# One more pair of token tiles by seven products in a linear-attention and SwiGLU kernel, with the small work around it moved between engines

## The chip, the core and the metric

The kernel runs on one core of a Trainium2 chip. The core has a matrix engine (TensorE, PE in the profile; its weight loads are shown apart as PEld), three engines for element-wise work (VectorE = DVE, ScalarE = ACT, GpSimd = POOL), and SyncE (SP), which only issues transfers here. Each engine works through its own list of instructions in order; semaphores make one engine wait for another. Matrix products land in PSUM, all other tiles lie in SBUF, and inputs, outputs and spill buffers in HBM.

The metric is the device time of one execution in microseconds (us): 748.28 for the kernel before, the median of three runs (747.86 to 748.52).

## The reference

`x` is 2048 tokens by 1024. It is normalised, and two blocks use the result: a linear attention with 32 heads of 32 columns, and a feed-forward block with a hidden width of 3584.

```python
xn = layernorm(x)                                    # over the 1024 columns, no weights
q, k, v = split(xn @ wqkv)                           # 32 heads of 32 columns each
phi = lambda t: where(t > 0, t + 1, exp(t)) + 1e-6
kv, z = sum_s phi(k)[s] (x) v[s],  sum_s phi(k)[s]   # per head: 32x32 and 32
num, den = phi(q) @ kv,  phi(q) . z + 1e-6
s = (num / den) @ wo
g = silu((silu(xn @ w_gate) * (xn @ w_up)) @ w_down)
out = x + s * g
```

The `1e-6` that is added to `den` is one of the operations that the change touches; `@ wo` is the output projection that it touches most.

## The kernel before

Tokens are handled in 16 tiles of 128, four tiles to a block of 512 (`TB`). The stages follow each other on TensorE:

1. Normalisation, keys and values (to about 155 us). Products of 128x128 weights with 512 columns; `kvz_ps` gathers `kv` and `z` of all heads.
2. Queries of the second half of the tokens (class `QGroup`, groups `qa`, `qb`, `qc`), woven into the start of stage 3. Each query group needs its results passed through `exp` and `relu` on ScalarE (`emit_exp_relu`, L186 and L187, four instructions per half group) and through a minimum and an addition on VectorE (`emit_phi`, L190 and L191, called by `part_d`, a "row").
3. num/den and output projection (about 156 to 232 us). For each of the 16 token tiles `nd_tile()` calls `emit_ND` (L779), and for each of 32 half rows `s_unit()` calls `emit_S` (L821).
4. The feed-forward block (from 232 us): groups of gate and up products (class `Group`), then the down projection.

Most large products are done in blocks of two by two with seven products in place of eight (the names `M1` to `M5`, `N6`, `N7`), which needs sums of the operands' blocks ahead (on VectorE) and three combining additions behind. A group has three parts: `part_a` computes `M3` into `X` and `M4` into `Y`, copies `X` to SBUF on ScalarE and adds `Y` on VectorE; `part_b` computes `M1` into `Z`, which is added to that sum, then accumulates `M5` onto `X` and `M2` onto `Y`; `part_c` accumulates `N7` and `N6` and subtracts. So `M5` may start only when the copy of `X` is done, and `M2` only when the addition has read `Y`.

What `emit_ND` issues for one tile: 8 products of 132 columns into three PSUM tiles `nd_ps` (three, three and two head groups), of which the pool `psA` has three buffers in all, so that the next call writes the same three; per PSUM tile an addition of 1e-6 to the denominators into `rden` (L794, VectorE); one reciprocal of `rden` (L797, VectorE); and per PSUM tile a multiplication into `o_sb` (L800, VectorE). `emit_OT` then stores `o_sb` to `o_dram` from ScalarE's queue (L815) and issues a transposing load into `oT` from SyncE's queue (L816); behind the last tile it also issues the first six weight loads of the feed-forward block (`load_w`, L177 and L179).

`emit_S` multiplies one transposed tile with half of `wo` (8 products of 512 columns), copies the result on ScalarE (L833) and, for the second half, stores the row to `s_dram` from ScalarE's queue (L836).

The last four token tiles are projected by seven products: class `SGroup` takes two tiles, its `sums()` makes four sums of their transposes on VectorE, and five sums of blocks of `wo` (`wo_sums`, 128x2048 each) are made once, on GpSimd (L959). The places for these sums are reused ones: halves of `oT` blocks whose tiles have been projected, and the upper half of `ws_all`.

The order around the change is written out by hand. The block at L921 runs under `manual_schedule` for TensorE, VectorE, ScalarE, GpSimd and SyncE, so each engine's list is the order in which the Python code emits. Before the loop come three `nd_tile()` calls between the parts of `qa` and `qb`, each followed by an `emit_OT()`. The loop over `u` counts the output-projection units; at each `u` it looks up whether a query part (`q_at`), a num/den tile (`nd_at`), a row (`row_at`), a sum of `wo` (`wo_at`) or the sums of the first group (`sum_at`) goes with it, then calls `s_unit()` and `emit_OT()`. In the feed-forward block only TensorE and GpSimd keep the written order; VectorE and ScalarE are ordered by the planner, and `gate(...)` ties an instruction behind another in that planning, without a semaphore unless `sync=True`. `sum_w(m, gu)` makes the four sums of a feed-forward weight block on VectorE (L152 to L155); `sum_w(0, 0)` and `sum_w(0, 1)` stand at the end of the block at L921.

Of the kernel before, what the change touches and what calls it, by code (L numbers as in the profile page):

```python
# [9 lines left out]
ACT = mybir.ActivationFunctionType  # L10
ALU = mybir.AluOpType
# [10 lines left out]
def kernel(  # L22
# [143 lines left out]
    def sum_w(m, gu):  # L166
        wsum[(m, gu)] = ws_all[:, m % 2, gu]
        for op in wsum_ops(wraw[(m, gu)], wsum[(m, gu)]):
            op()

# [18 lines left out]
    def emit_phi(dst, e):  # L189
        nc.vector.tensor_scalar(out=e, in0=e, scalar1=1.0, scalar2=EPS, op0=ALU.min, op1=ALU.add)  # L190
        marks["phi"] = nc.vector.tensor_tensor(out=dst, in0=e, in1=dst, op=ALU.add)  # L191

# [563 lines left out]
    with ExitStack() as p2:  # L756
        wop = p2.enter_context(tc.tile_pool(name="wop", bufs=1, reuse_waits="tile"))
        otp = p2.enter_context(tc.tile_pool(name="p2oT", bufs=1))
        work = p2.enter_context(tc.tile_pool(name="p2work", bufs=2))
        small = p2.enter_context(tc.tile_pool(name="p2small", bufs=2))  # L760
        oT_ab = otp.tile([P, 2, G, TB], BF16, name="oT")
        oT_cd = wq_sb[:].rearrange("p c n -> p (c n)").rearrange("p (b g t) -> p b g t", b=2, t=TB)
# [3 lines left out]
        def oT_of(b):  # L766
            return (oT_ab[:] if b < 2 else oT_cd)[:, b % 2]
# [11 lines left out]
        def emit_ND(b, t):  # L779
# [4 lines left out]
            for j in range(NJ):  # L784
                g0 = j * GPT
                ng = min(GPT, G - g0)
                nd_ps = psA.tile([P, GPT, NDW], FP32, name="nd_ps", tag="A")
                for gi in range(ng):
                    g = g0 + gi
                    mm = nc.tensor.matmul(nd_ps[:, gi, :], lhsT=pqT_tiles[(p, g // 2)][:, g % 2, t0:t0 + P],  # L790
                                          rhs=KVZ[:, g, :], start=True, stop=True)
                    if j == 0 and gi == 0 and t == 0:
                        marks[("ND", b)] = mm
                nc.vector.tensor_scalar(out=rden[:, g0:g0 + ng, :], in0=nd_ps[:, 0:ng, P:P + HPG],  # L794
                                        scalar1=EPS, scalar2=None, op0=ALU.add)
                nds.append((g0, ng, nd_ps))
# [13 lines left out]

        def emit_OT():
            while o_ready:
                b, t, o_sb = o_ready.popleft()
# [7 lines left out]
        def emit_S(b, t, cc):  # L821
# [12 lines left out]
            if cc == NCC - 1:  # L834
# [9 lines left out]
        wos += [oT_ab[:, 1, 0:HD]]  # L844
        wo_sums = deque((out, u, v, op) for out, (u, v, op) in zip(wos, (
            (w12, w22, ALU.subtract), (w21, w11, ALU.subtract), (w11, w22, ALU.add), (w21, w22, ALU.add),
# [4 lines left out]
                  oT_cd[:, 0, 0:1].rearrange("p a (k c) -> p (a k) c", k=HD)]  # L851
        o_sums = [oT_ab[:, 1, HD:DC], oT_cd[:, 0, HD:DC]]

        class SGroup:


            def __init__(self, t):
                self.t = t
                o = oT_of(NB - 1)[:, :, t * P:(t + 2) * P]
                a, b = o[:, :, 0:P], o[:, :, P:2 * P]  # L860
                self.o, self.s1, self.sum = o, o_sum1[t // 2], o_sums[t // 2]
                s1, sm = self.s1, self.sum
# [19 lines left out]
            def store(self, i):  # L882
                r0 = ((NB - 1) * TPB + self.t + i) * P
                nc.scalar.dma_start(out=s_dram[r0:r0 + P, :], in_=self.s[i][:])
# [32 lines left out]
        def nd_tile():  # L917
            if nds:
                emit_ND(*nds.popleft())

        with tc.manual_schedule(engines=FRONT_ORDER | {ET.SP}):  # L921
# [18 lines left out]
            rows = deque((grp, i) for grp in (qa, qb, qc) for i in range(2))  # L940
            nd_at = {1, 2, 4, 6, 8, 10, 11, 13, 15, 16, 17, 19, 20}
            row_at = {0, 1, 3, 5, 7, 9}
            wo_at = {10, 11, 12, 14, 18}
            sum_at = {23: lambda: groups[0].sums()}
            q_at = {0: qc.part_a, 2: qc.part_b, 3: qc.part_c}
            assert len(nd_at) == len(nds) and len(row_at) == len(rows)
            n7 = TPB * NCC
            groups = [SGroup(t) for t in range(0, TPB, 2)]
            for u in range(len(units) - n7):
                if u in q_at:  # L950
                    q_at[u]()
                if u in nd_at:
                    nd_tile()
                if u in row_at:
                    grp, i = rows.popleft()
                    grp.part_d(i)
                if u in wo_at:
                    out, a, b, op = wo_sums.popleft()
                    gate([nc.gpsimd.tensor_tensor(out=out, in0=a, in1=b, op=op)], marks["phi"], sync=True)  # L959
                if u in sum_at:  # L960
                    sum_at[u]()
                s_unit()
                emit_OT()
            sg, sh = groups
            sg.part_a()
            sh.sums()
            sg.part_b()
# [4 lines left out]
            sh.part_c()  # L972
            sum_w(0, 1)
    p12.close()
# [209 lines left out]
    with tc.manual_schedule(engines=PE_ORDER):  # L1184
        prev = None
        for m, p in order:
# [15 lines left out]
            for gu in range(2):  # L1202
# [14 lines left out]
                grp.part_b()  # L1217
                prev = grp
                if p == 0 and m + 1 < NM:
                    sum_w(m + 1, gu)  # L1220
                if gu == 0 and (m, p) in wd_at:
# [126 lines left out]
```

## Time and profile before

| | before |
|---|---|
| median of 3 runs | 748.28 us (747.86 to 748.52) |
| profiled execution | 747.96 us |
| its span, first to last instruction | 746.2 us |
| granted TensorE clock | 0.999 |

The work of the engines by stretch of the span, in us of busy time (the profile's table by stretches):

| stretch, us | PE | DVE | ACT | POOL | DMA share |
|---|---|---|---|---|---|
| 0 to 70, normalisation, keys and values | 68.08 | 57.15 | 32.41 | 14.04 | 0.78 |
| 70 to 143, the same with query groups | 72.69 | 58.60 | 43.82 | 0 | 0.01 |
| 143 to 161 | 17.95 | 14.40 | 10.01 | 0 | 0.38 |
| 161 to 212, num/den and projection | 50.68 | 39.67 | 22.10 | 20.13 | 0.65 |
| 212 to 232, last projection groups | 19.89 | 12.64 | 6.43 | 0 | 0.97 |
| 232 to 400, feed-forward | 167.17 | 125.45 | 65.13 | 0 | 0.53 |
| 400 to 568 | 168.00 | 119.38 | 65.02 | 0 | 0.57 |
| 568 to 746.2, down projection and end | 172.45 | 90.14 | 27.37 | 35.74 | 0.45 |

A line of the timeline has the start in us, the duration, engine, source line, operation, the tiles written and read, their sizes and the number of instructions that the line merges; in brackets stands how long the engine was idle before it and what ended that. Matmuls overlap: four of 512 columns that follow each other start 0.216 us apart, though each is listed with 0.38 us. A few matmul records are missing, so that a merged line can count 7 where 8 ran. "ACTq" and "SPq" are the queues' issue of transfers.

### The profile page before, as it was taken

The numbers are of one execution on the slowest core, as the hardware profiler recorded it, in microseconds if no ns is written. First come the engines' busy times: TensorE is split into PE (matmuls) and PEld (weight loads), VectorE is DVE, ScalarE is ACT, GpSimd is POOL, SyncE is SP. The second block draws the span as 40 slices with busy tenths as digits, with TensorE's granted clock in tenths as the row PEclk, the third lists the DMA queues.
The fourth block names the chain that finished last, engine by engine and source line by source line (L and its number), as shares of the span: only waits on it lengthen the run. The fifth ranks groups of instructions, "written<-read, shape, count | busy, mean of one in ns | idle before, by whom it ended". The sixth has DMA issues, their size and how long they took to land.

```text
span 746.2 us, 9886 instructions
## 1 busy us (share of the span) xinstructions
PE 736.9 (99%) x3661; PEld 347.0 (47%) x3700; DVE 517.4 (69%) x955; ACT 272.3 (36%) x476; POOL 69.9 (9%) x106
## 2 busy tenths in 40 slices
PE   9999999999999999999999999999999999999997
PEld 4544444455544444444444444444444444444454
DVE  6889896688768767787678867776655754445554
ACT  4444574755223343434343333434342111111111
POOL 3210000000730000000000000000000221121220
PEclk9999999999999999999999999999999999999999
DMA  9756000316689553655337643455779745554200
GB/s 313 260 161 170 1 0 1 113 44 156 198 230 278 149 149 101 188 174 158 109 97 204 184 127 105 150 161 156 265 255 344 284 171 183 184 184 170 98 29 29
DMA packets 132464, 118.09 MB, mean 158 GB/s; under 512 B 33728, under 2 KB 112704, under 8 KB 131136
## 3 DMA queue, kind: packets, MB, share of 16 engines
q1 hardware_dynamic: 127520, 108.68, 47.1%
q10 hardware_dynamic: 4896, 8.78, 3.5%
q8 instruction: 29, 0.48, 0.3%
q14 instruction: 19, 0.16, 0.1%
HBM read 70.52 MB, written 39.58 MB: 148 GB/s over the span
## 4 chain that ended last, share of the span: by engine, by line
PE 96%; DMA 2%; DVE 1%; issue 0%; ACT 0%; DVEq 0%; ACTq 0%
PE X L131 29%; PE Y L131 29%; PE Z L131 10%; PE kv_ps L455 9%; PE s_ps L829 5%; PE qX L131 3%; PE qY L131 3%; PE kY L131 2%; PE kX L131 2%; DMA wg_sb<-in_B_w_gate_dram 1%; PE nd_ps L790 1%; PE kvz L484 1%; PE qZ L131 1%; PE kZ L131 1%; DMA xp<-in_A_x_dram 0%
## 5 line engine op out<-in xcount | busy, mean ns | idle before, releaser
L131 PEld LDWEIGHTS <-ws_all 128*128 128x128 bf16 x1424 | 138.1, 98 | 164.0 <-issue 1.9
L1011 DVE TENSOR_TENSOR q<-n,Y 128x512 f32<-128x512 f32 x63 | 43.3, 688 | 104.4 <-PE Y L131 103.2
L131 PEld LDWEIGHTS <-xs 128*128 128x128 bf16 (+1 forms) x736 | 69.6, 98 | 76.5
L1281 POOL TENSOR_TENSOR o_out<-y,xres 128x512 bf16<-128x512 f32 x29 | 35.1, 1210 | 495.1 <-DVE y L1280 495.1
L131 PE MATMUL Y<-xs,ws_all 128*128 128x512 f16 (+3 forms) x308 | 70.3, 360 | 0.0
L131 PE MATMUL X<-xnT,ws_all 128*128 128x512 f16 (+1 forms) x278 | 70.1, 379 | 0.2
L131 PE MATMUL Y<-xnT,ws_all 128*128 128x512 f16 x224 | 57.5, 379 | 0.8 <-DVE q L1011 0.8
L131 PE MATMUL X<-xs,ws_all 128*128 128x512 f16 x224 | 57.5, 379 | 0.0
L131 PE MATMUL Z<-xs,ws_all 128*128 128x512 f16 x224 | 57.5, 379 | 0.0
L1135 ACT ACTIVATE g<-cg 128x512 bf16<-128x512 f32 x56 | 35.3, 630 | 54.4 <-DVE cg L1026 54.4
L1017 DVE TENSOR_TENSOR u<-Z,q 128x512 f32<-128x512 f32 x63 | 43.2, 686 | 15.9 <-PE Z L131 15.9
L1135 ACT ACTIVATE g<-X 128x512 bf16<-128x512 f32 x28 | 16.7, 597 | 99.0 <-PE X L131 99.0
L1007 ACT COPY n<-X 128x512 f32<-128x512 f32 x63 | 36.9, 585 | 30.8 <-PE X L131 27.6
L455 PEld LDWEIGHTS <-xnT 128*128 128x128 f16 x320 | 30.7, 98 | 36.0 <-DVE xnT L427 0.5
L1160 DVE TENSOR_TENSOR ho<-g,up 128x1024 bf16<-128x1024 bf16 x56 | 38.2, 685 | 0.5
L455 PE MATMUL kv_ps<-wk_sb,xnT 128*128 128x512 bf16 x156 | 36.9, 379 | 0.6 <-DVE xnT L427 0.3
L1280 DVE TENSOR_TENSOR y<-y,s_in 128x512 f32<-128x512 f32 x31 | 22.2, 717 | 21.4 <-ACT y L1274 15.8
L455 PE MATMUL kv_ps<-wv_sb,xnT 128*128 128x512 bf16 x155 | 35.9, 379 | 0.2
L131 PEld LDWEIGHTS <-wu_sb 128*128 128x128 bf16 x224 | 21.9, 98 | 26.4
L131 PEld LDWEIGHTS <-wg_sb 128*128 128x128 bf16 x224 | 21.9, 98 | 26.4
L1274 ACT ACTIVATE y<-X 128x512 f32<-128x512 f32 x8 | 4.8, 597 | 69.7 <-PE X L131 61.2
L829 PE MATMUL s_ps<-wo_sb,oT 128*128 128x512 bf16 x123 | 29.0, 379 | 0.2
(208 smaller groups left out, 1146.8 us busy)
## 6 DMA issues: line engine op xcount, KB each, us to landing
h_dram<-ho SPq DMA_DIRECT2D x56, 256.0 KB, 2.5
wg_sb<-in_B_w_gate_dram SPq DMA_DIRECT2D x14, 512.0 KB, 4.0
wu_sb<-in_B_w_up_dram SPq DMA_DIRECT2D x14, 512.0 KB, 4.4
wdr<-in_B_w_down_dram SPq DMA_DIRECT2D x14, 512.0 KB, 4.2
ws_all<-h_dram SPq DMA_DIRECT2D x4, 1792.0 KB, 8.7
wds_dram<-wdsA SPq DMA_DIRECT2D x14, 384.0 KB, 2.7
hp_a<-h_dram SPq DMA_DIRECT2D x3, 1792.0 KB, 9.6
o_dram<-o_sb ACTq DMA_DIRECT2D x16, 256.0 KB, 3.1
```

Source lines behind the costliest of these rows:

```text
L131: marks["mm"] = nc.tensor.matmul(acc[:, 0:c1 - c0], lhsT=lhs(k), rhs=rhs(k)[:, c0:c1], start=(first and k == 0), stop=(k == n - 1), skip_g ...
L455: mm = nc.tensor.matmul(kv_ps[:], lhsT=xn_tok_ap(i)[:, dc, :], rhs=wkv_ap(c)[:, dc, :], start=(dc == 0), stop=(dc == DC - 1))
L484: nc.tensor.matmul(kvz_ps[j][:, gi, 0:P + 1], lhsT=pk_sb[:, g * P:(g + 1) * P], rhs=v_sb[:, g, 0:P + 1], start=(i == 0 and gi == 0), stop= ...
L790: mm = nc.tensor.matmul(nd_ps[:, gi, :], lhsT=pqT_tiles[(p, g // 2)][:, g % 2, t0:t0 + P], rhs=KVZ[:, g, :], start=True, stop=True)
L829: mm = nc.tensor.matmul(s_ps[:], lhsT=oT[:, c, ttok], rhs=wo_sb[:, c, cc * CW:(cc + 1) * CW], start=(c == 0), stop=(c == G - 1))
L1007: nc.scalar.copy(out=n[:], in_=self.X[:])
L1011: nc.vector.tensor_tensor(out=self.q[:], in0=n[:], in1=self.Y[:], op=ALU.add)
L1017: nc.vector.tensor_tensor(out=self.u[:], in0=Z[:], in1=self.q[:], op=ALU.add)
L1135: nc.scalar.activation(out=self.g[:, i, j * TB:(j + 1) * TB], in_=src, func=ACT.Silu)
L1160: nc.vector.tensor_tensor(out=self.ho[:, i], in0=self.g[:, i], in1=self.up[:, i], op=ALU.mult)
L1280: nc.vector.tensor_tensor(out=t[:], in0=t[:], in1=self.s_in[:, i, cs], op=ALU.mult)
L1281: (nc.vector if last and (i, j) != (0, 0) else nc.gpsimd).tensor_tensor(out=self.o_out[:, i, cs], in0=t[:], in1=self.xres[:, i, cs], op=AL ...
```

## The change

Five things are changed together.

- The projection of the third last pair of token tiles (tiles 10 and 11) is done by `SGroup` as well: `S7 = 3` groups in place of two, so 20 units remain in the loop in place of 24. The three groups are called `sf`, `sg`, `sh`. The places for their sums alternate between two.
- The 1e-6 is added to the denominators on ScalarE: an `activation` with function `Identity` and a bias tile `eps_nd`, which GpSimd fills once.
- The five sums of `wo` are made on VectorE, at other units (`wo_at`), and without the `gate` to the last row.
- The num/den tiles and the rows come at other units (`nd_at`, `row_at`), the last tile at `u` = 18 of 20 in place of 20 of 24; `emit_OT` moves from behind `s_unit()` to behind `nd_tile()`, and there handles only the tiles that were ready before that `nd_tile()`.
- `sum_w(0, 1)` moves out of the block into the feed-forward loop, behind `part_b` of the first group, and it and both `sum_w(1, gu)` are gated behind the last matmul issued there.

```diff
     def sum_w(m, gu):
         wsum[(m, gu)] = ws_all[:, m % 2, gu]
-        for op in wsum_ops(wraw[(m, gu)], wsum[(m, gu)]):
-            op()
+        return [op() for op in wsum_ops(wraw[(m, gu)], wsum[(m, gu)])]
...
+        eps_nd = small.tile([P, 1], FP32, name="eps_nd", tag="eps_nd", bufs=1)
+        nc.gpsimd.memset(eps_nd[:], EPS)
...
-                nc.vector.tensor_scalar(out=rden[:, g0:g0 + ng, :], in0=nd_ps[:, 0:ng, P:P + HPG],
-                                        scalar1=EPS, scalar2=None, op0=ALU.add)
+                nc.scalar.activation(out=rden[:, g0:g0 + ng, :], in_=nd_ps[:, 0:ng, P:P + HPG], func=ACT.Identity,
+                                     bias=eps_nd[:])
...
-        def emit_OT():
-            while o_ready:
+        def emit_OT(n=None):
+            for _ in range(len(o_ready) if n is None else n):
...
+        S7 = 3
...
-            def __init__(self, t):
-                self.t = t
-                o = oT_of(NB - 1)[:, :, t * P:(t + 2) * P]
+            def __init__(self, n):
+                self.t = NT - 2 * (S7 - n)
+                t = self.t % TPB
+                o = oT_of(self.t // TPB)[:, :, t * P:(t + 2) * P]
                 a, b = o[:, :, 0:P], o[:, :, P:2 * P]
-                self.o, self.s1, self.sum = o, o_sum1[t // 2], o_sums[t // 2]
+                self.o, self.s1, self.sum = o, o_sum1[n % 2], o_sums[n % 2]
...
-            nd_at = {1, 2, 4, 6, 8, 10, 11, 13, 15, 16, 17, 19, 20}
-            row_at = {0, 1, 3, 5, 7, 9}
-            wo_at = {10, 11, 12, 14, 18}
-            sum_at = {23: lambda: groups[0].sums()}
+            nd_at = {1, 2, 4, 5, 7, 9, 10, 11, 13, 14, 15, 17, 18}
+            row_at = {0, 1, 3, 5, 6, 8}
             q_at = {0: qc.part_a, 2: qc.part_b, 3: qc.part_c}
+            wo_at = {6: (2,), 8: (3,), 12: (0,), 16: (1, 4)}
...
+                done = len(o_ready)
                 if u in nd_at:
                     nd_tile()
+                emit_OT(done)
                 if u in row_at:
                     grp, i = rows.popleft()
                     grp.part_d(i)
-                if u in wo_at:
-                    out, a, b, op = wo_sums.popleft()
-                    gate([nc.gpsimd.tensor_tensor(out=out, in0=a, in1=b, op=op)], marks["phi"], sync=True)
-                if u in sum_at:
-                    sum_at[u]()
+                for k in wo_at.get(u, ()):
+                    out, a, b, op = wo_sums[k]
+                    nc.vector.tensor_tensor(out=out, in0=a, in1=b, op=op)
+                if u == len(s_order) - 1:
+                    groups[0].sums()
                 s_unit()
-                emit_OT()
-            sg, sh = groups
+            sf, sg, sh = groups
+            sf.part_a()
+            sg.sums()
+            sf.part_b()
             sg.part_a()
+            sf.part_c()
             sh.sums()
             sg.part_b()
             sh.part_a()
             sg.part_c()
             sum_w(0, 0)
             sh.part_b()
             sh.part_c()
-            sum_w(0, 1)
...
                 grp.part_b()
                 prev = grp
+                if (m, p, gu) == (0, 0, 0):
+                    gate(sum_w(0, 1), marks["mm"])
                 if p == 0 and m + 1 < NM:
-                    sum_w(m + 1, gu)
+                    sums = sum_w(m + 1, gu)
+                    if m == 0:
+                        gate(sums, marks["mm"])
```

## The prediction

> **What bounds the kernel now.** I read the page's busy times and its chain first, then TensorE's waits, then the timeline of 156 to 238 us, where the change lies.
>
> ```profile
> PE 736.9 (99%) x3661; PEld 347.0 (47%) x3700; DVE 517.4 (69%) x955; ACT 272.3 (36%) x476; POOL 69.9 (9%) x106
> PE 96%; DMA 2%; DVE 1%; issue 0%; ACT 0%; DVEq 0%; ACTq 0%
> ```
>
> TensorE bounds every stage. So a product that goes is worth its own spacing, and work on another engine costs nothing until TensorE waits for it: the question is which wait is new. TensorE waits for little today; the largest wait is at the start of the feed-forward block:
>
> ```profile
> 232.93 1.03 PE L131 MATMUL Y<-xs,wg_sb 128*128 128x512 f16 x4
> 233.91 1.02 PE L131 MATMUL Z<-xs,ws_all 128*128 128x512 f16 x4
> 234.30 0.58 ACT L1007 COPY n<-X 128x512 f32<-128x512 f32 x1 [3.25 <-PE Y L131]
> 234.94 1.02 PE L131 MATMUL X<-xnT,ws_all 128*128 128x512 f16 x4
> 236.05 0.68 DVE L1011 TENSOR_TENSOR q<-n,Y 128x512 f32<-128x512 f32 x1
> 236.79 1.02 PE L131 MATMUL Y<-xnT,ws_all 128*128 128x512 f16 x4 [0.83 <-DVE q L1011]
> ```
>
> Four matmuls follow each other in 4 x 0.216 = 0.86 us; here the three products come 0.12, 0.17 and 0.99 us late, 1.27 in all. VectorE reaches `q` late because sums of feed-forward weights (L152 to L155) stand ahead of it.
>
> The num/den tiles are tight too. TensorE's next tile writes the `nd_ps` buffers that VectorE's multiplications of this one read:
>
> ```profile
> 160.43 0.63 PE L790 MATMUL nd_ps<-KVZ,pqT 128*128 128x132 bf16 x8
> 160.49 0.63 ACT L186 ACTIVATE e_t<-pqT 128x512 bf16<-128x512 bf16 x1 [1.86 <-DVE pqT L251]
> 161.24 0.31 DVE L794 TENSOR_SCALAR rden<-nd_ps 128x12 f32<-128x12 f32 x3
> 161.97 1.35 DVE L800 TENSOR_TENSOR o_sb<-nd_ps,rden 128x384 bf16<-128x384 f32 x3
> 162.33 0.63 ACT L187 ACTIVATE pqT<-pqT 128x512 bf16<-128x512 bf16 x1
> 163.49 0.63 PE L790 MATMUL nd_ps<-KVZ,pqT 128*128 128x132 bf16 x8
> ```
>
> Tile 1's multiplications end at 163.32, 0.17 us ahead of tile 2's products. And ScalarE, which is to add the 1e-6, is busy with the query group's four exp/relu until 162.96. Where two tiles stand one unit apart, TensorE waits already (0.77 in place of 0.63 us), and ScalarE copies and stores the previous unit in between:
>
> ```profile
> 203.83 0.77 PE L790 MATMUL nd_ps<-KVZ,pqT 128*128 128x132 bf16 x8
> 204.03 0.58 ACT L833 CAST s_sb<-s_ps 128x512 bf16<-128x512 f32 x1 [1.61 <-PE s_ps L829]
> 204.20 0.59 DVE L794 TENSOR_SCALAR rden<-nd_ps 128x12 f32<-128x12 f32 x3
> 204.64 0.33 ACTq L836 DMA_DIRECT2D s_dram<-s_sb  x1
> 205.22 1.35 DVE L800 TENSOR_TENSOR o_sb<-nd_ps,rden 128x384 bf16<-128x384 f32 x3
> 206.15 0.76 PE L790 MATMUL nd_ps<-KVZ,pqT 128*128 128x132 bf16 x8
> ```
>
> **The change part by part.** Order on each engine is the code's own.
>
> *Third pair by seven products.* 32 matmuls become 28: -4 x 0.216 = -0.86 us. Its sums and combining steps (four sums, 1.7 us; three additions and two subtractions in place of copies) run on VectorE beside 6 us of products each. `sg.sums` overwrites places that `sf.part_a` reads, and is needed 6 us later; `sh` writes the `s_sb` buffers that `sf` stores from, whose stores go out 8 us before; stores at 227.78 us landed after 5.8. So 0 here; if the store is late ScalarE's copy waits, and behind it the next product (a rival below).
>
> *Weight sums later.* `q` and `u` come ahead of the eight sums (3.3 us), which are needed about 4 us after `u` at the earliest: the 1.27 us go, -1.27. Weight loads are issued behind the last transposing load; from tile 15's num/den to the feed-forward block TensorE now has 19.7 us (212.40 to 232.07), then about 21.6, so SyncE's queue is earlier and hides them.
>
> *1e-6 on ScalarE.* 48 instructions leave VectorE (0.46 us a tile) and 48 come to ScalarE. No row shows this operation there. The nearest is the square root of 128x1 from SBUF with a bias tile, 0.296 us; exp of 128x512 takes 0.63 from SBUF and 0.597 from PSUM, so I take 0.26 for PSUM, and 0.16 from start to start, since exps from PSUM follow each other at 0.495, 0.10 under their length. Ends: VectorE's 0.17 and 0.12 for the same operation; 0.296 without overlap. GpSimd's memset waits for buffers of the stage before; ScalarE's first use is at 157.8, 2 us after anything it can wait for.
>
> By the Trainium skill, "ScalarE: Activation LUTs", section "What ACT_TABLE_LOAD costs", an activation with a bias pointer takes about 280 ns + 0.833 ns a column and overlaps the next by 93 ns: 0.29 and 0.197 us as an estimate; by it the whole sum would be +5.9 in place of +5.1 us. The 0.296 row agrees with it; the two exp rows, 33 ns apart, do not let me use it unchanged for PSUM.
>
> More than its length it is the place that costs. Replaying the rows' durations in the new order:
>
> Tile 2. Tile 0's additions now follow ScalarE's relu that starts at 157.29: 157.8 to 158.4, reciprocal at 158.4, not 157.38. VectorE is 1.0 late, so the query group's subtractions and ScalarE's four exp/relu are too: they start at 161.5 and pass at 163.9. Only then come tile 1's additions: reciprocal 164.5 (was 161.59), multiplications ending 165.45, 165.9 and 166.25. Tile 2's products, due at 163.49, run at 165.5 to 166.4 in place of ending at 163.99: +2.45 us.
>
> Tile 6, now one unit behind tile 5 (2.2 us, was 3.9). In ScalarE's list tile 5's additions stand behind `qc`'s four exp/relu, the copy of unit 3 and its store: with the rows at 178 to 181.4 that is 2.2 us behind tile 5's first product. Additions 0.58, reciprocal 0.35, multiplications 0.56, 0.47, 0.42 more; tile 6's third buffer is free at +4.5, due at +2.55: +1.99 us.
>
> Tile 8 needs the last query row. Row and tile 8 keep their distances of one unit to tile 7 and to each other, which left 0.18 us (191.28 to 191.46). Tile 7's additions follow a copy and the sum of `wo` at unit 6 (1.22 us): +0.69 on the last products.
>
> Tiles 9, 10, 12, 13 and 15 stand one unit behind another. For 12: ScalarE's copy ends 0.78 behind tile 11's first product, additions 0.78 to 1.36, reciprocal to 1.75, multiplications to 2.35, 2.8 and 3.15; the buffers are due at 2.2, 2.37 and 2.55: +0.65. In the same way 9, 10, 13 and 15 come to 0.59, 0.48, 0.41 and 0.65; together +2.78.
>
> Today's waits in this stretch go, since the sums above count from the undelayed spacing: four of 0.126 at num/den tiles, and 0.19 at `qb`'s `N7` and `N6`: -0.69.
>
> *Sums of wo on VectorE.* 5 x 1.22 us (the 128x2048 rows at L510) in place of 5 x 4.07 on GpSimd, off TensorE's path but for the part in tile 8 above; the two at unit 16 end ahead of tile 14's reciprocal.
>
> *Order of stores.* `o_sb` stores now stand behind the next tile's additions, about 0.7 us later on ScalarE's queue; transposing loads on SyncE's follow them. Tiles 10 and 11 are read 14 us or more after their products; tile 13 was read from SBUF after 11 today. 0; without that cover a late transposition would stop TensorE one for one.
>
> Sum: -0.86 - 1.27 - 0.69 + 2.45 + 1.99 + 0.69 + 2.78 = +5.09. The profiled execution took 747.96 us (span 746.2 and 1.76 around it): 753.05, and the median of the runs stands 0.32 above it: 753.4. With the low price of an addition the same replay gives +3.8, with the high one +7.3: 752.1 to 755.6.
>
> **Rivals.** *Faster:* the additions on ScalarE end no later than VectorE's did, 0.87 us after a tile's first product. Then the 0.46 us that VectorE saves cover the rest and only the savings stay: -2.82, 745.5. It decides if ScalarE's backlog ahead of tiles 1 and 5 is gone when their products end; the rows at 160.49 to 162.96 speak against it.
>
> *Half:* an addition costs 0.1 us and 0.05 from start to start: +2.3, 750.6. Every row on ScalarE speaks against it.
>
> *No change:* the pile-ups behind exp/relu (tiles 2 and 6) hide, the pairs cost what I say: 5.09 - 4.44 = +0.65, 748.9.
>
> *More:* TensorE's gaps of 2 us bring its clock down. At the start of the span matmuls follow each other 0.427 us apart for 3.2 us; eight such more per gap, 0.211 each, at two gaps: +3.4, 756.8. Against it: the 0.99 us wait at 236.79 is followed by 0.216 spacing. By the Trainium skill, "TensorE: Matmul & The Clock Gate", Part 1, the clock halves after an idle window of about 3.4 us, and no gap here is so long. A late `sf` store, 1 us, would end in the same region.
>
> **How the numbers follow.** Mine 0.75; faster 0.07; half 0.06; no change 0.05; more 0.07. Changes within 0.2% (1.5 us) count as none, which is about what a measurement can tell here. Faster 0.07, same 0.05, slower 0.88. The range 750.5 to 756.0 takes in the ends of the addition's price and the half case, and leaves out the rest, under 0.2.
>
> **What would show it.** Right: in the changed profile TensorE waits for `o_sb` at L790's line, over 1.5 us at tiles 2 and 6; `rden` on ScalarE starts behind L187; no wait for `q` at the first feed-forward group; the stretch from 156 us to the first `M3` of the feed-forward block longer by 6.4 us. Wrong: `rden` well under 0.2 us, or ScalarE free when the products of tiles 1 and 5 end.

## The result and the profile after

The changed kernel took 755.88 us in the median of six executions (753.57 to 760.25) against 748.37 us for the kernel before beside it. The ratio is 1.0111, with an interval of 1.0092 to 1.013: slower by 1.1%, which on the 748.28 us of the table is 756.6 us. The forecast was 753.4 us with a range up to 756.0. The direction was right; the size was not, by 3 us.

The recorded profile is that of the fastest of the six: 753.57 us, span 751.8 us, 5.61 us more than the profiled execution before. The forecast for a profiled execution was 753.05. So the profile shows an execution in which the forecast sum came out nearly as worked, and the typical execution has some 2 us more that this profile does not show. Both halves need an explanation.

The page of the changed kernel, busy times and chain:

```profile
PE 738.2 (98%) x3658; PEld 346.0 (46%) x3696; DVE 520.3 (69%) x920; ACT 280.6 (37%) x523; POOL 50.0 (7%) x102
PE 94%; DVE 3%; ACT 2%; issue 1%; ACTq 0%; DVEq 0%
```

TensorE still bounds the span, but VectorE and ScalarE now hold 5% of the chain (1% before), and 1% is issue. The waits of TensorE in the same profile (columns: what waited, for whom, us in total, times, longest):

```profile
PE nd_ps L791 <- DVE o_sb L801: 3.9, 2, 2.0
PE nd_ps L791 <- DVE pqT L190: 0.4, 1, 0.4
```

The two long waits are those of tiles 2 and 6. The timeline at tile 1 and tile 2 (start, duration, engine, line, operation, tiles):

```profile
160.21 0.63 PE L791 MATMUL nd_ps<-KVZ,pqT 128*128 128x132 bf16 x8
...
163.07 0.63 ACT L186 ACTIVATE pqT<-pqT 128x512 bf16<-128x512 bf16 x1
163.61 0.57 ACT L795 ACTIVATE rden<-nd_ps,eps_nd 128x12 f32<-128x12 f32 x3
...
164.21 0.35 DVE L798 RECIPROCAL rden<-rden 128x32 f32<-128x32 f32 x1 [2.42 <-ACT rden L795]
...
164.67 1.35 DVE L801 TENSOR_TENSOR o_sb<-nd_ps,rden 128x384 bf16<-128x384 f32 x3
...
165.28 1.08 PE L791 MATMUL nd_ps<-KVZ,pqT 128*128 128x132 bf16 x8 [1.85 <-DVE o_sb L801]
```

Tile 1's products start at 160.21, but its additions follow the query group's last relu and start 3.4 us later; before, VectorE had added 0.81 us behind the products (160.43 to 161.24). VectorE sits idle 2.42 us for `rden`, and tile 2's products come 2.44 us late (2.016 us ahead of the first, 0.278 and 0.150 between the groups). The pair that was shown before, tiles 11 and 12, in the timeline after:

```profile
206.90 1.09 PE L791 MATMUL nd_ps<-KVZ,pqT 128*128 128x132 bf16 x8
206.92 0.58 ACT L834 CAST s_sb<-s_ps 128x512 bf16<-128x512 f32 x1 [1.12 <-PE s_ps L830]
207.54 0.33 ACTq L837 DMA_DIRECT2D s_dram<-s_sb  x1
207.92 0.27 ACT L795 ACTIVATE rden<-nd_ps,eps_nd 128x12 f32<-128x12 f32 x1 [0.41 <-PE nd_ps L791]
...
208.99 1.35 DVE L801 TENSOR_TENSOR o_sb<-nd_ps,rden 128x384 bf16<-128x384 f32 x3
209.60 1.09 PE L791 MATMUL nd_ps<-KVZ,pqT 128*128 128x132 bf16 x8
```

Eight matmuls that took 0.77 us now take 1.09, and the next tile comes 2.70 us after this one where it came after 2.32 us. The start of the feed-forward block:

```profile
240.19 0.58 ACT L1015 COPY n<-X 128x512 f32<-128x512 f32 x1 [2.27 <-PE X L131]
240.66 1.03 PE L131 MATMUL Z<-xs,ws_all 128*128 128x512 f16 x4
240.93 0.69 DVE L1019 TENSOR_TENSOR q<-n,Y 128x512 f32<-128x512 f32 x1 [1.19 <-PE Y L131]
241.52 1.03 PE L131 MATMUL X<-xnT,ws_all 128*128 128x512 f16 x4
242.38 1.03 PE L131 MATMUL Y<-xnT,ws_all 128*128 128x512 f16 x4
```

`q` ends at 241.62, 0.76 us ahead of the product that writes `Y` again; before, that product started 0.06 us behind `q`, after a wait of 0.83. Now the products follow each other at 0.86 us.

By stretch, from TensorE's starts in the two profiles: up to the first num/den products nothing moved (149.29 and 149.27 us from the first key/value products); from there to the feed-forward block's first product 75.56 became 82.56, +7.00; from there to the last matmul 509.27 became 508.09, -1.18.

### The profile page after: what moved, and what is told of

Same layout as the page of the kernel before. It is cut to its first block, busy times and chain, and to the rows that moved or that the text cites. A ratio compares the mean times of both kernels' runs of the same rounds, so it can differ in the third digit from the quotient of the medians.

```text
span 751.8 us, 9888 instructions
## 1 busy us (share of the span) xinstructions
PE 738.2 (98%) x3658; PEld 346.0 (46%) x3696; DVE 520.3 (69%) x920; ACT 280.6 (37%) x523; POOL 50.0 (7%) x102
## 4 chain that ended last, share of the span: by engine, by line
PE 94%; DVE 3%; ACT 2%; issue 1%; ACTq 0%; DVEq 0%
PE X L131 29%; PE Y L131 29%; PE Z L131 10%; PE kv_ps L454 9%; PE s_ps L830 3%; PE qY L131 2%; PE qX L131 2%; PE kY L131 2%; PE kX L131 2%; DVE o_sb L801 1%; PE sX L131 1%; PE sY L131 1%; PE kvz L483 1%; PE qZ L131 1%; PE w_ps L492 1%; PE nd_ps L791 1%
```

## The experiments

The forecast's theory is that the additions on ScalarE are the whole loss, by what stands ahead of them in ScalarE's order. What it left open after the result is the part beyond the profile. The theory for that is the rival "More": long gaps halve TensorE's clock for a while, in some executions and not in others. Its own rival was a late store. In all runs below the kernel before ran beside them: 747.84 us in the median for the first four (23 executions), 747.96 for the next four (17, from the one longer gap to the version with the stores later), 747.86 for the last three (21).

### The changed kernel again

No edit.

> The changed kernel unchanged, for more executions with their granted clocks. The recorded profile was the fastest of six executions (753.57 us, clock 1.000); the other five took 754.47 to 760.25 at 0.999 to 0.995. Theory A (the two gaps of about 2.5 us at num/den tiles 2 and 6 bring TensorE's clock down in some executions): the fastest executions stand at 753 to 754 with clock 1.000, the others above by (1 - clock) x 752 us, and a profile with a lower clock shows it low right behind 165 or 186 us. Theory B (late transposing loads or weight loads make the spread): the times spread at a clock of 1.000, and the profile shows waits for DMA on TensorE.

755.58 us (754.45 to 759.5); ratio 1.0109, interval 1.0091 to 1.0128. This time the profile is of a 756.40 us execution, and it has what the first had not. The table by stretches (us; busy time and instructions of each engine; granted clock; DMA), four neighbouring stretches around tile 2's products:

```profile
core 0: us, PE busy (x) PEld busy (x) DVE busy (x) ACT busy (x) POOL busy (x), PEclk, DMA share, GB/s
160.60:164.00 3.40, 3.40 (x23) 1.77 (x22) 2.17 (x5) 1.77 (x3) 0.00 (x0) 1.00 0.24 81
164.00:167.40 3.40, 1.43 (x12) 0.58 (x11) 2.11 (x5) 3.06 (x9) 0.00 (x0) 1.00 0.18 42
167.40:170.80 3.40, 3.40 (x10) 1.20 (x9) 2.69 (x7) 0.91 (x4) 0.00 (x0) 0.50 0.70 118
170.80:174.20 3.40, 3.40 (x19) 1.63 (x18) 1.23 (x3) 2.56 (x5) 0.00 (x0) 1.00 0.58 154
```

Behind the stretch in which TensorE stood for tile 2, the granted clock is 0.50 for 3.413 us, and then 1.00 again. Matmuls of 512 columns follow each other 0.427 us apart there in place of 0.216; eight fit, so one such stretch costs 8 x 0.211 = 1.7 us. The profile of the first run had the same gap and no such stretch. Against that first profile the way from tile 0 to the feed-forward block is 1.87 us longer: 1.7 for the clock, 0.77 for a wait at 239.97 us (below), less 0.64 that tile 6's wait is shorter, since TensorE reaches it later. The start of the program took 1.1 us more as well, ahead of everything that the change touches: the granted clock first rises at 6.98 us here and at 4.73 in the first profile. So the clock is the largest part of the 2.8 us between the two executions, and not all of it.

### 1e-6 back on VectorE

```diff
-        eps_nd = small.tile([P, 1], FP32, name="eps_nd", tag="eps_nd", bufs=1)
-        nc.gpsimd.memset(eps_nd[:], EPS)
...
-                nc.scalar.activation(out=rden[:, g0:g0 + ng, :], in_=nd_ps[:, 0:ng, P:P + HPG], func=ACT.Identity,
-                                     bias=eps_nd[:])
+                nc.vector.tensor_scalar(out=rden[:, g0:g0 + ng, :], in0=nd_ps[:, 0:ng, P:P + HPG],
+                                        scalar1=EPS, scalar2=None, op0=ALU.add)
```

> The changed kernel with one part undone: the 1e-6 is added on VectorE again. No backlog of exp/relu lies ahead of the additions. Theory A: the gaps at tiles 2 and 6 go; what is left are about 1.0 at tile 8, 1.0 at tile 9 and 0.65 at tile 15 from the sums of wo on VectorE, +0.6 against the kernel before (748.9 us), with a clock of 0.999 to 1.000 in every execution. Theory B: the spread of several us stays, since loads and stores are as they were.

748.51 us (748.08 to 753.29); ratio 1.0016, interval 1.0005 to 1.0027. One part of the change makes 7.1 of the 7.7 us. Tile 2 has no wait left, and tile 6 one of 0.12 us, as four tiles of the kernel before have. What is left besides is 0.46 us at tile 15, and 0.78 at tile 8 and 0.98 at tile 9, where VectorE now does two sums of `wo`, 1.22 us each, right at the last query row.

The profile fell on the slowest of the twelve executions, 753.29 us, and shows a wait that the prediction had priced at nothing. The timeline at the third group of the projection, with the same columns:

```profile
228.83 2.11 SPq L178 DMA_DIRECT2D wu_sb<-in_B_w_up_dram  x1
...
231.28 3.17 ACTq L885 DMA_DIRECT2D s_dram<-s_sb  x2
...
234.54 0.58 ACT L902 CAST s_sb<-sX 128x512 bf16<-128x512 f32 x1 [6.43 <-DMA wu_sb<-in_B_w_up_dram]
...
235.18 1.47 PE L131 MATMUL sX<-ws_all,oT 128*128 128x512 bf16 x4 [2.51 <-ACT s_sb L902]
```

`sg`'s two stores stand on ScalarE's queue ahead of `sh`'s copies. The second is not issued until 234.12, just behind the landing of a load of feed-forward weights at 234.02: in the program's list of waits the store and the load share a semaphore, since transfers take these in turn. `sh`'s copy stands behind the store and `sh`'s `N7` behind the copy, 2.67 us late. And that gap halves the clock (table by stretches, columns as above):

```profile
232.20:235.60 3.40, 0.89 (x5) 0.29 (x3) 0.81 (x2) 1.06 (x2) 0.00 (x0) 1.00 1.20 300
235.60:239.00 3.40, 3.40 (x10) 1.19 (x8) 1.30 (x2) 0.02 (x1) 0.00 (x0) 0.50 1.12 341
```

In the profile of the changed kernel run again the same wait is the 0.77 us at 239.97; in its first profile it is absent. It depends on when a load lands, so it differs by execution.

### The additions on ScalarE for the early or for the late tiles only

```diff
+                if b * TPB + t >= 7:
                     nc.scalar.activation(...)
+                else:
+                    nc.vector.tensor_scalar(...)
```

> The changed kernel with the 1e-6 on VectorE for tiles 0 to 6 and on ScalarE from tile 7 on: no query group's exp/relu stand ahead of any ScalarE addition. Theory A: the two long gaps go, the short ones (0.4 to 0.65 us at tiles 8, 9, 10, 12, 13, 15, 3.2 in all) stay; +0.9 against the kernel before, 749.2 us, and the clock holds at 0.999 to 1.000. If many short gaps bring the clock down rather than two long ones, this spreads as the changed kernel does. Theory B: spreads.

> The complement: the 1e-6 on ScalarE for tiles 0 to 5, on VectorE from tile 6 on. Theory A: the two long gaps stay (about 2.45 and 2.2 us at tiles 2 and 6); fastest executions at +4.7, 753.0 us, the others higher by up to 6 us at clocks of 0.995 to 0.999, as with the changed kernel. If short gaps do it: the clock holds and all executions stand within 1 us of 753.0.

Here the late tiles are 7 to 15, the early ones 0 to 5 (with `< 6`). Late tiles only: 749.29 us (748.99 to 750.29), ratio 1.0023, interval 1.0015 to 1.0032; no single gap of over 0.51 us behind the first num/den product, and no half clock before the last matmul. Early tiles only: 754.5 us (753.25 to 754.78), ratio 1.0086, interval 1.0073 to 1.0099; 2.45 us at tile 2, 1.96 at tile 6, and in the profiled execution (754.66 us) a stretch of 3.413 us at half clock behind tile 2. Against the additions wholly on VectorE the late tiles add 0.8 us and the early ones 6.0. The early ones' two waits are worth 4.4; the stretch at half clock, 1.7, makes 6.1. The four executions do not all fit this: one took 754.34 us at a mean clock of 1.000, and what made it long was not traced. The pairs behind one another wait as long as forecast with the late additions on ScalarE (tiles 9, 10, 12, 13 and 15: 2.79 us in sum, and 0.51 at tile 8). But with the additions on VectorE the same tiles wait 1.78 and tile 8 waits 0.78, so that only 0.75 us of all this is the price of ScalarE (0.8 by the medians); most of the rest is that of `wo`'s sums on VectorE at tiles 8 and 9.

### One gap, longer and shorter, in the kernel before

Only the additions of tiles 0 and 1, or only those of tile 1, go to ScalarE in the kernel before; nothing else is changed.

```diff
+        eps_nd = small.tile([P, 1], FP32, name="eps_nd", tag="eps_nd", bufs=1)
+        nc.gpsimd.memset(eps_nd[:], EPS)
...
+                if b * TPB + t < 2:       # the other one: == 1
+                    nc.scalar.activation(out=rden[:, g0:g0 + ng, :], in_=nd_ps[:, 0:ng, P:P + HPG], func=ACT.Identity,
+                                         bias=eps_nd[:])
+                else:
                     nc.vector.tensor_scalar(...)
```

> The kernel before with one thing added: the 1e-6 of tiles 0 and 1 alone is added on ScalarE. By the replay one gap at tile 2 of 2.1 + 0.29 + 0.16 us, all inside 2.9 us, and nothing else: +2.3 us. In the profiles so far the clock record changes only at multiples of 3.413 us, and a stretch at half clock lasts 3.413 us, which costs 1.7 us. Theory A (a gap of about 2.4 us halves the clock for one such period when it falls into one period, else not): executions in two heaps, at +2.3 and at +4.0 us, the clock lower by 0.002 in the upper. Theory B (only the loads and stores at the end of the projection make the spread): one heap at +2.3, clock as before.

> The same for tile 1 alone: the gap at tile 2 is 1.06 + 0.29 + 0.16 us, +1.3 us. Theory A: too short, so one heap at +1.3 us and the clock as before. If any gap of over 1 us brings the clock down: two heaps, at +1.3 and +3.0. Theory B: one heap.

The long gap (2.028 us, with 0.43 us between the groups behind it): 752.0 us, in two heaps. Two executions took 749.65 and 750.13 us with a mean clock of 1.000; four took 751.95 to 753.36 with 0.996 or 0.997. The profiled one, 750.13, is of the first heap, 2.2 us above the kernel before for a gap of 2.46. The short gap (1.417 us, with 0.43 behind it): 749.3 us, eleven executions from 748.82 to 749.7 with clocks of 0.998 to 1.000, one heap, 1.3 us above the kernel before for a gap of 1.85. So a gap 0.6 us longer costs 0.4 to 0.8 us more in some executions and 2.7 to 4.1 in others. One period at half clock accounts for 1.7 of the 2.3 us between the middles of the two heaps; the rest was not traced. No execution of the upper heap was profiled, so that it had such a period is read from its mean clock. The clock also falls once behind the last matmul, so this mean is 0.998 to 1.000 in the profiles that have no period at half clock before that; 0.996 and 0.997 lie below it.

What goes with a fall of the clock is seen when its changes are set against the gaps. In every trace the clock changes only at whole multiples of 3.413 us from its first rise (in the changed kernel run again, from 6.98 to 167.41 us is 47 of them). The idle time of TensorE inside one such period, worked out from the matmuls' starts with 0.216 us allowed for each of 512 columns, in the fullest period of each profile:

| profile | idle of 3.413 us | clock in the next period |
|---|---|---|
| before, start of the feed-forward block | 1.24 | 1.0 |
| short gap | 1.42 | 1.0 |
| long gap | 1.49, the rest in the next | 1.0 |
| after, tile 2 | 1.89, the rest in the next | 1.0 |
| GpSimd sums (below), tile 6 | 1.93 | 1.0 |
| stores later (below), tile 2 | 2.17 | 0.5 |
| additions of the early tiles, tile 2 | 2.32 | 0.5 |
| after again, tile 2 | 2.44 | 0.5 |
| additions on VectorE, late store | 2.67 | 0.5 |
| GpSimd sums, tile 8 | 3.41 | 0.5 |

Up to 1.93 us of a period nothing happens; from 2.17 the next period runs at half clock. Tile 2's gap of 2.4 us lies above that if it falls within one period, and below if a period's edge cuts it, as in the first profile of the changed kernel, whose edge lies at 165.16, inside the gap. The periods run on their own: the first rise came between 4.33 and 7.18 us in these profiles.

### The sums of wo on GpSimd, where the change has them

This was meant to beat both kernels: additions on VectorE (the edit of "1e-6 back on VectorE"), and on top of it the five sums of `wo` on GpSimd at the change's units.

```diff
-                    nc.vector.tensor_tensor(out=out, in0=a, in1=b, op=op)
+                    nc.gpsimd.tensor_tensor(out=out, in0=a, in1=b, op=op)
```

> The changed kernel with the 1e-6 on VectorE and the sums of wo on GpSimd again, so that the third pair by seven products, the earlier num/den tiles, the order of stores and the later weight sums remain. By the replay waits of 0.12 at six tiles and 0.18 at qb remain, 0.9 in all: -1.9 us against the kernel before. Theory A: clock as before, but the stores of sg, which wait on ScalarE's queue for the landing of weight loads (eps_dve's profile: issue at 234.12, the load landed at 234.02), can still stop sh's copies, so single executions up to 2.7 us + 1.7 us above. Theory B says the same of these single executions, and nothing of the changed kernel's median.

A miss: 759.17 us (756.87 to 759.73), ratio 1.0146, interval 1.0129 to 1.0162. The timeline at the last query row:

```profile
190.98 8.23 POOL L962 TENSOR_TENSOR oT<-wo_sb 128x2048 bf16<-128x2048 bf16 x2 [8.29 <-DVE rden L796]
192.16 3.16 DVE L189 TENSOR_SCALAR e_t<-e_t 128x1024 bf16<-128x1024 bf16 x1
...
195.42 4.35 DVE L190 TENSOR_TENSOR pqT<-e_t,pqT 128x1024 bf16<-128x1024 bf16 x1
...
199.82 0.29 PE L789 MATMUL nd_ps<-KVZ,pqT 128*128 128x132 bf16 x1 [5.98 <-DVE pqT L190]
```

A row's two VectorE instructions take 0.42 and 0.69 us where no sum runs on GpSimd. Beside GpSimd's sums each ends just behind one of them: at 195.32 and 199.77, where the two sums, 4.1 us each from 190.98, end at 195.03 and 199.22. The same happens once more earlier: the first instruction of a row that starts at 179.63 takes 3.35 us and ends at 182.98, beside a sum from 178.63 to 182.70, and tile 6 waits 2.67 us for it in all. Tile 8's last product waits 6.1 us for the row, a whole period of 3.413 us is idle, and the clock stays at half for two periods (6.827 us). The VectorE instructions beside GpSimd that read PSUM kept their length, the multiplications their 1.35 us for three.

With `sg`'s two stores besides issued behind `sh`'s copies:

```diff
-            sg.part_c()
+            sg.part_c(stores=False)
             sum_w(0, 0)
             sh.part_b()
+            sg.store(0)
+            sg.store(1)
             sh.part_c()
```

(`part_c` with `stores=False` leaves out its own two stores.)

> best, with sg's two stores issued behind sh.part_b's copies in place of ahead of them. If the late stores make the single slow executions, they are gone: all executions at -1.9 us against the kernel before, within 0.6 us. If they are something else (the time from the start to the first product), they stay.

758.11 us (757.76 to 759.02), ratio 1.014, interval 1.0127 to 1.0153: the same two gaps, and the wait of 0.84 us at `sh`'s copies is gone. That part did what it was meant to; it could not mend the row.

### GpSimd's sums held until the last row is done

The kernel with the stores later (the last run above), with the sums at units 9, 10, 12 and 16, each gated behind the last row as the kernel before had them.

```diff
-        nc.vector.tensor_tensor(out=dst, in0=e, in1=dst, op=ALU.add)
+        marks["phi"] = nc.vector.tensor_tensor(out=dst, in0=e, in1=dst, op=ALU.add)
...
-            wo_at = {6: (2,), 8: (3,), 12: (0,), 16: (1, 4)}
+            wo_at = {9: (2,), 10: (3,), 12: (0,), 16: (1, 4)}
...
-                    nc.gpsimd.tensor_tensor(out=out, in0=a, in1=b, op=op)
+                    gate([nc.gpsimd.tensor_tensor(out=out, in0=a, in1=b, op=op)], marks["phi"], sync=True)
```

> The changed kernel with 1e-6 on VectorE, sg's two stores issued behind sh's copies, and wo's five sums on GpSimd, each held until the last phi row has been added (as before had them), at units 9, 10, 12 and 16. Theory: in the two versions without that hold, GpSimd's first sums (8.2 us for two) ran beside the last row's two VectorE instructions and stretched them from 0.42 and 0.69 us to 3.16 and 4.35 us, so TensorE stood 6.1 us and the clock was halved twice (3.4 us more). Behind the hold no row is left to stretch: about -1.9 us against the kernel before, 746.0 us (745.4 to 747.0), no half clock in the record and the last row's instructions at 0.42 and 0.69 us. Rival: GpSimd's sums are simply too slow for three pairs (5 sums of 4.1 us); then the products that read them wait and it stays over 749 us.

746.47 us (745.97 to 748.37), ratio 0.9985, interval 0.9976 to 0.9994: 1.4 us under the kernel before and 9.1 under the changed one. The timeline at the last row:

```profile
188.58 0.42 DVE L189 TENSOR_SCALAR e_t<-e_t 128x1024 bf16<-128x1024 bf16 x1
189.10 0.69 DVE L190 TENSOR_TENSOR pqT<-e_t,pqT 128x1024 bf16<-128x1024 bf16 x1
189.93 8.07 POOL L963 TENSOR_TENSOR ws_all<-wo_sb 128x2048 bf16<-128x2048 bf16 x2 [145.84 <-PE s_ps L828]
190.07 0.46 DVE L793 TENSOR_SCALAR rden<-nd_ps 128x12 f32<-128x12 f32 x3 [0.28 <-PE nd_ps L789]
```

GpSimd starts when the row has ended, both of the row's instructions have their usual length, and the clock does not fall ahead of the last matmul. GpSimd is not too slow for three groups either: the five sums take 4.1 us each and none of them is waited for. Units and hold changed together here. But without the hold GpSimd's first sum, put at unit 6, began at 166.69 us, ahead of tile 3's products, so the unit alone does not keep it back.

### The stores alone, and the weight sums alone

The changed kernel with `sg`'s stores behind `sh`'s copies and nothing else:

> The changed kernel with sg's two stores issued behind sh's copies and nothing else touched. Theory: the late stores cost the changed kernel 0 to 2.7 us by execution, 0.8 us in the profile that showed them: median 754.8 us (753.5 to 755.5), and no wait at sh's copies near 240 us. Rival (stores cost nothing, as the prediction had it): 755.6 us, as the changed kernel.

753.8 us (753.65 to 755.82, four executions), ratio 1.0088, interval 1.0074 to 1.0102: 1.8 us under the 755.58 of the changed kernel in an earlier comparison. `sh`'s copies keep no product waiting in the profile. It came 1 us lower than expected. With four executions of which only one, the profiled one of 755.82 us, is shown by its trace to have a period at half clock, the median is likely that of executions without; the other three took 753.65 to 753.81. How much of the 1.8 us is the store's and how much is chance in where the periods fell stays open.

The kernel before with the later weight sums alone (`sum_w` returns its instructions, as in the change):

```diff
-            sum_w(0, 1)
...
+                if (m, p, gu) == (0, 0, 0):
+                    gate(sum_w(0, 1), marks["mm"])
                 if p == 0 and m + 1 < NM:
-                    sum_w(m + 1, gu)
+                    sums = sum_w(m + 1, gu)
+                    if m == 0:
+                        gate(sums, marks["mm"])
```

> The kernel before with the later weight sums of the feed-forward alone: the second sum (0,1) and the next two behind the feed-forward's first products, and nothing else touched. Theory (the prediction's term of -1.27 us for the waits at the feed-forward's start): 746.6 us (746.3 to 747.2). Rival: the wait at the start is set by something else that is late next: 747.9 us.

746.85 us (746.34 to 747.76), ratio 0.9988, interval 0.9979 to 0.9997: 1.0 us under the kernel before beside it, for 1.27 forecast; in the profiles the way from the block's first product to the last matmul is 1.26 us shorter (508.01 for 509.27). Of the 1.4 us that the best version gains, this part has most. In the timeline `q` and `u` now come ahead of the sums, and the fifth product of the block follows the fourth at 0.86 us:

```profile
233.88 0.69 DVE L1009 TENSOR_TENSOR q<-n,Y 128x512 f32<-128x512 f32 x1 [1.10 <-ACT n L1005]
234.49 1.03 PE L131 MATMUL X<-xnT,ws_all 128*128 128x512 f16 x4
...
235.35 1.03 PE L131 MATMUL Y<-xnT,ws_all 128*128 128x512 f16 x4
235.35 0.42 DVE L152 TENSOR_TENSOR ws_all<-wu_sb 128x512 bf16<-128x512 bf16 x1
```

## Why the prediction was right and wrong

The steps, against the first profile of the changed kernel, which has no period at half clock:

| step | forecast, us | measured, us |
|---|---|---|
| waits at the feed-forward block's start | -1.27 | -1.18 |
| tile 2 | +2.45 | +2.44 |
| tile 6 | +1.99 | +2.60 |
| tile 8 | +0.69 | +0.60 |
| tiles 9, 10, 12, 13, 15 | +2.78 | 0.68 + 0.41 + 0.60 + 0.48 + 0.61 = +2.78 |
| tile 0 to the feed-forward block | +6.4 | +7.00 |
| the profiled execution | +5.09 | +5.61 |

That this execution came within 0.52 us of the sum is in part luck: the edge of a period cut its gap at tile 2, and no store was late in it.

*Right.* The price of an addition on ScalarE was 0.26 us, and 0.16 from start to start; the 48 take 0.252 to 0.308, 0.272 in the middle, and three follow each other in 0.57 to 0.61 where nothing holds them up. That the place in ScalarE's order costs more than the length is shown twice: by the rows at 163.07 and 163.61, and by the two half versions, where the same additions cost 0.8 us for the nine late tiles and 6.0 for the six early ones, which stand behind exp/relu. The savings came as well: the later weight sums alone gain 1.0 us.

*Tile 6*, mis-sized by 0.6: its additions stand behind the exp/relu, a copy and a store, as written. In the changed kernel run again, where TensorE comes to it after a period at half clock, the wait was 1.96 us, so part of what TensorE loses ahead of it is won back there. Most of what the replay missed stands in the first profile: tile 5's additions start 2.67 us behind its first product (184.49 and 181.82) in place of the 2.2 of the replay. Tile 4's additions, on ScalarE too, kept VectorE waiting 1.09 us, and with it the exp/relu ahead of tile 5's additions: these start 1.05 us behind the output-projection product of unit 3 where they started 0.06 behind it before.

*The step that failed* is the one from the profiled execution to the median: "the median of the runs stands 0.32 above it", and with it the rejection of the rival "More", which had 0.07. The sentence used against it was that "the 0.99 us wait at 236.79 is followed by 0.216 spacing". That is true, but a wait of 0.99 us says nothing of one of 2.4: the waits of the prediction's own replay at tiles 2 and 6 were longer than anything in the trace of before. The other ground was that no gap reaches the 3.4 us of an idle window. The Trainium skill, "TensorE: Matmul & The Clock Gate", Part 1, says that the clock halves after an idle window of about 3.4 us and that the window is free-running, 3413 ns long; it does not say how much of the window has to be idle, and the prediction took it to be all of it. The traces agree with the length (3.413 us) and with its running freely, and show that 2.17 us idle of it is enough.

"More" had the right mechanism and a price near it: 1.7 us for each gap, 756.8 in all. What happens lies between: an execution has none of these periods, one, or more, by where the periods' edges fall. The mean clocks fit this. Of the twelve executions of the changed kernel in the two comparisons, three at 0.999 or 1.000 took 753.57 to 754.47 us, six at 0.997 or 0.998 took 755.0 to 756.4, and three at 0.995 took 758.97 to 760.25. The medians, 755.88 and 755.58, lie in the middle group, whose traced execution, 756.40, has one such period. One period lowers the mean by 3.413 x 0.5 / 752 = 0.0023, and the fall behind the last matmul by up to 0.002, so 0.995 would be about two periods, an estimate; they would make 3.4 of the 6.7 us between the fastest and the slowest, and the rest was not traced. How the clock and the late store below share the excess of the median stays open. That a gap alone can do it is what the kernel before with one long gap shows: nothing else was changed there, and in its profile no product waits behind a store.

*The second failed step* is "So 0 here" for the stores of the groups. The rival sentence "a late `sf` store, 1 us" named the right kind of wait but the wrong store: it is `sg`'s, its cause is the landing of a feed-forward weight load, and it costs 0 in one profile, 0.77 in another and 2.67 in a third. To price it, the waits of each store on ScalarE's queue should have been followed to transfers on SyncE's queue.

*A right sum with a wrong share.* The 0.69 and 0.59 us of tiles 8 and 9 were put down mostly to the additions. With the additions on VectorE these two tiles still wait 0.78 and 0.98 us, with the sums of `wo` of units 6 and 8 on VectorE's list ahead of the row and of tile 8's additions. The version with the sums on GpSimd behind the last row, and the stores later, is 2.0 us faster than the one with additions and sums on VectorE (746.47 and 748.51; how much of it is the stores' was not separated); the term "off TensorE's path but for the part in tile 8 above" was too small.

## What to carry to other kernels

Before an operation goes to an engine that seems free, list what stands ahead of it on that engine at that moment: here instructions of 0.27 us cost 4.4 us of waits at two tiles because of the four exp/relu ahead of them, and 6.0 in all (the version with the early tiles alone). A new wait of 2 us or more on TensorE can cost 1.7 us on top of itself in some executions, by the clock, and one profile, above all of the fastest execution, does not show which. An instruction order that looks like needless caution, such as sums held behind a row, may be what keeps two engines out of each other's way: undo it alone before judging it.

## What the runs showed of the hardware that was not expected

- In all thirteen profiles the clock changes only at whole multiples of 3.413 us from its first rise, which came between 4.33 and 7.18 us. 1.93 us idle in one such period left the clock at 1.0, 2.17 us halved it for the next (1.7 us lost). Where the limit lies between was not tried. After a wholly idle period it stayed at half for two periods; TensorE still stood for some 1.5 us of the first of them, and whether that or the whole idle period makes the second was not tried.
- A VectorE instruction of 128x1024 bf16 that reads SBUF alone, beside a GpSimd sum of 4.1 us that reads SBUF, did not end until that sum did: 3.16 and 3.35 in place of 0.42 us and 4.35 in place of 0.69. VectorE instructions that read PSUM kept their length beside the sums, and so did the small reciprocal (128x32 f32, 0.35 us), which reads SBUF alone. The Trainium skill, "SBUF — State Buffer", "Who interferes with whom", says that a VectorE instruction with two SBUF inputs contends with a GpSimd instruction that reads SBUF, that one in a two-port mode, which `tensor_scalar` can enter, contends as well, and that one with at most one SBUF input outside these modes does not. The row of 4.35 us, with two SBUF inputs, and the rows that read PSUM agree; whether the rows of 3.16 and 3.35 us, with one SBUF input, ran in a two-port mode no trace shows.
- A store on ScalarE's queue waited for the landing of a load on SyncE's that has nothing to do with it, up to 2.67 us on TensorE's path: they share a semaphore in this program, the load landed at 234.02 us and the store was issued at 234.12 (238.81 and 238.91 in the changed kernel run again).
